# A reordered front end for a fused routed-attention and SwiGLU kernel: keys ahead of queries, odd-token one-hots put off, weights in column quarters, dummy products between the first exponentials

## The chip, the cores and the metric

The kernel runs on one core of one Trainium2 chip. The metric is the device time of one execution in microseconds (us). Every kernel was run several times. The profiles are single executions, and their spans are about 1.8 us shorter than the time of the same run, because the time includes a little before and after the span.

The engines in the profile are PE (TensorE's products), PEld (its weight loads), DVE (the vector engine), ACT (the scalar engine), POOL (GpSimd) and SP (the engine that here only issues transfers). "PEclk" is the clock granted to TensorE, 1.00 being full speed and 0.50 half speed.

## The reference

There are 4 batches, 8 heads, 768 tokens and a head width of 64. Each query and each key is assigned to one of 16 centroids of its head, by the largest cosine. A query attends only to keys with the same assignment. The result is normalised (RMS) and goes through a SwiGLU layer with 512 inputs and 1536 hidden columns.

```python
q_assign = argmax(einsum('bhsd,hcd->bhsc', q_n, c_n), axis=-1)   # k_assign likewise
mask = q_assign[:, :, :, None] == k_assign[:, :, None, :]
scores = where(mask, scale * q @ k.T, -1e9)
attn = softmax(scores) @ v
x = attn.transpose(0, 2, 1, 3).reshape(B * S, H * D)
xn = x / sqrt(mean(x * x) + 1e-6) * rms_g
out = (silu(xn @ w_gate) * (xn @ w_val)) @ w_out
```

## The kernel before

The mask costs no separate pass. To each query and key (64 rows after transposition) 16 more rows are added, a one-hot vector of the assignment, so that a product over 80 rows is large exactly where the assignments agree, and one exponential with a constant offset gives the masked weights. Producing these rows is the "preparation" of a head: load q and k, transpose them on TensorE (`trans`), copy to SBUF on ACT, multiply with the centroids (`scores_c`), find the maximum and compare on DVE, transpose back, and place the one-hots by a small DMA (`place`). `qcast` and `kcast` write the bf16 rows of query and key. Heads are prepared in groups of four.

The work is cut into 8 units, each half the tokens of one batch with all 8 heads. "Even" and "odd" tokens are the two halves; unit 0 uses only the even queries of batch 0, but all its keys. In unit u the attention of u runs (24 exponentials of 128x768), and beside it, as fill, the feed-forward work of earlier units and the preparation of later groups. The order of instructions on each engine is exactly the order of the program text.

```python
def load_gv(c):                       # gate and value weights, four row blocks
    nc.gpsimd.dma_start(out=wg[:, c], in_=moe_w_gate[c * P:(c + 1) * P])
    nc.gpsimd.dma_start(out=wv[:, c], in_=moe_w_val[c * P:(c + 1) * P])
...
def kcast(g, h, early=False):
    for e in range(2):
        to, of = kext[g % 4][:D, h, e * UQ:(e + 1) * UQ], qkT[g, h // 2][e * D:(e + 1) * D, h % 2, 1]
        if early:
            nc.scalar.activation(to, of, ACT.Copy, scale=1.0 / ZS)
        else:
            nc.vector.tensor_scalar_mul(to, of, 1.0 / ZS)
...
def group_work(g):                    # preparation of one group of four heads
    w = []
    for h in range(HG):
        ...
        def second(h=h, n=n):
            trans(g, h, 1)
            qcast(g, h)
            kcast(g, h)
            vcast(n)
            load_qk(n + NQ)
            load_v(n + NV)
        w.append((0.25, second))
...
def second_group():                   # runs between exponentials 2 and 3 of unit 0
    kcast(0, 2, True)
    kcast(0, 3, True)
    for m in range(2):
        scores_c(1, m)
    for c in range(CC):
        load_gv(c)
    ...
...
for u in range(NU):
    ...
    elif u == 1:
        prep = group_work(2) + group_work(3)
        fill += [(0.5, f) for _, f in prep[:8]] + ffn[:12] + [(0.0, output_weights)] + spread(ffn[12:], prep[8:])
    ...
            while n < len(fill) and (h, i) > (0, 0) and done <= total * (3 * h + i + 1) / gaps:
                done += fill[n][0]
                fill[n][1]()
                n += 1
```

The softmax here doesn't subtract the row's maximum and nothing guards it: scores larger than these inputs give would overflow.

## Time and profile before

| | before |
|---|---|
| time, median of 3 runs | 375.29 us (373.96 to 375.66) |
| profiled span | 371.76 us |
| first exponential | 18.82 us |
| last exponential of unit 0 ends | 44.81 us |
| normalised x of unit 0 complete | 53.55 us |
| first gate product | 58.40 us |
| key 11, the last load of group 2, lands | 51.41 us |
| starts of units 2 to 6 | 87.53, 129.85, 171.68, 213.51, 255.35 us |

These are lines of the page of the kernel before: the busy time of each engine with its instruction count; the busy share of TensorE and its clock in 40 slices of 9.3 us each (a digit 9 is 90% or more); the packets that the transfers were made of, by size; and two of the DMA issues, with the size of a transfer and the median time from issue to landing.

```profile
PE 351.1 (94%) x3026; PEld 210.5 (57%) x3026; DVE 241.7 (65%) x573; ACT 260.0 (70%) x461; POOL 107.6 (29%) x221
...
PE   7979867999999999999999999999999999999995
...
PEclk9976998999999999999999999999999999999999
...
DMA packets 24967, 32.03 MB, mean 86 GB/s; under 512 B 4960, under 2 KB 20832, under 8 KB 24928
...
wv<-in_moe_w_val_dram POOLq DMA_DIRECT2D x4, 384.0 KB, 10.3
wo<-in_moe_w_out_dram POOLq DMA_DIRECT2D x3, 512.0 KB, 13.5
```

Read the PE row first. From the eighth slice on TensorE is never under 90% but in the last one, so only the first seven slices, some 65 us, hold slack. The clock row has its own dip, in slices three and four (19 to 37 us), where the PE row shows 7 and 9: busy there means slow as well. The weight transfers are not urgent in this kernel: all gate and value weights are in by 44.54 us, and the output weights, issued at 55 us, are needed only in unit 2.

### The profile page before, as it was taken

What the parts mean: (1) busy time and instruction counts of PE and PEld (TensorE: products, weight loads), DVE (VectorE), ACT (ScalarE), POOL (GpSimd) and SP (SyncE); (2) the same over time, 40 slices, a digit from 0 to 9 for tenths busy, and PEclk for the clock granted to TensorE, in tenths of its full rate; (3) what the DMA queues carried; (4) which work ended last, traced back from release to release, by engine and by line L of the source; (5) the groups of instructions that cost most, each with busy time, mean ns of one, the idle gap of its engine ahead of it and who ended that gap; (6) DMA issues with size and microseconds to landing.
All of it is one profiled execution on the core that took longest, in us unless ns stands there. A gap on an engine that the chain in (4) does not pass through costs nothing.

```text
span 371.8 us, 8016 instructions
## 1 busy us (share of the span) xinstructions
PE 351.1 (94%) x3026; PEld 210.5 (57%) x3026; DVE 241.7 (65%) x573; ACT 260.0 (70%) x461; POOL 107.6 (29%) x221
## 2 busy tenths in 40 slices
PE   7979867999999999999999999999999999999995
PEld 3535544565566555655566555655566656664552
DVE  4981186678756966777756966777656565667432
ACT  4797983798669775888668775888767876762320
POOL 3694071089615170325315170325300000000000
PEclk9976998999999999999999999999999999999999
DMA  8649999726126101450022001000020002001002
GB/s 273 188 95 210 249 329 248 159 63 180 58 85 198 63 20 56 129 155 14 13 85 86 4 20 57 30 0 13 12 86 2 3 0 86 2 1 58 28 3 85
DMA packets 24967, 32.03 MB, mean 86 GB/s; under 512 B 4960, under 2 KB 20832, under 8 KB 24928
## 3 DMA queue, kind: packets, MB, share of 16 engines
q1 hardware_dynamic: 18288, 24.72, 20.5%
q0 software_dynamic: 6064, 6.00, 8.6%
q10 hardware_dynamic: 576, 0.79, 0.6%
q8 instruction: 24, 0.39, 0.4%
q14 instruction: 15, 0.12, 0.1%
HBM read 28.35 MB, written 6.29 MB: 93 GB/s over the span
## 4 chain that ended last, share of the span: by engine, by line
PE 71%; ACT 12%; DVE 11%; issue 3%; DMA 1%; DVEq 0%; SPq 0%; ACTq 0%
PE o L370 17%; PE gate L347 13%; PE val L347 13%; PE s L280 13%; PE acc L296 7%; ACT pT L282 7%; PE tq L196 3%; PE sc L251 3%; DVE th L356 2%; ACT th L355 2%; DVE kext L210 2%; ACT qkT L198 1%; ACT xn L315 1%; DVE oh L242 1%; DVE o_sb L373 1%
## 5 line engine op out<-in xcount | busy, mean ns | idle before, releaser
L282 ACT ACTIVATE pT<-s,off 128x768 bf16<-128x768 f32 x192 | 170.9, 902 | 48.3 <-PE s L280 47.3
L280 PE MATMUL s<-qext,kext 80*128 80x384 bf16 x384 | 96.6, 335 | 5.6 <-ACT pT L282 5.2
L347 PE MATMUL val<-xnT,wv 128*128 128x384 bf16 x384 | 78.7, 327 | 0.9 <-DVE th L356 0.6
L347 PE MATMUL gate<-xnT,wg 128*128 128x384 bf16 x384 | 78.9, 327 | 0.1
L370 PE MATMUL o<-wo,gvT 128*128 128x512 bf16 x288 | 70.3, 379 | 0.5
L356 DVE SCALAR_TENSOR_TENSOR th<-th,gate 128x384 f32<-128x384 f32 x84 | 46.4, 553 | 30.3 <-ACT th L355 29.2
L280 PEld LDWEIGHTS <-kext 80*128 80x128 bf16 x384 | 37.2, 100 | 45.2 <-issue 18.5
L202 POOL CAST qext<-qkT 64x384 bf16<-64x384 f32 x64 | 33.7, 526 | 97.2 <-ACT qkT L198 95.3
L355 ACT ACTIVATE th<-gate 128x384 f32<-128x384 f32 x84 | 41.2, 490 | 25.9 <-PE gate L347 22.0
L361 DVE SCALAR_TENSOR_TENSOR gvT<-th,val 128x384 bf16<-128x384 f32 x84 | 46.3, 552 | 9.1 <-PE val L347 2.6
L296 PEld LDWEIGHTS <-pT 128*128 128x128 bf16 x1152 | 44.9, 99 | 9.7 <-issue 0.8
L347 PEld LDWEIGHTS <-wv 128*128 128x128 bf16 x384 | 36.5, 98 | 23.7 <-issue 3.2
L347 PEld LDWEIGHTS <-wg 128*128 128x128 bf16 x384 | 36.6, 98 | 22.7 <-issue 0.7
L296 PE MATMUL acc<-vbf,pT 128*128 128x65 bf16 x1152 | 47.0, 195 | 0.5 <-ACT pT L282 0.5
L370 PEld LDWEIGHTS <-gvT 128*128 128x128 bf16 x288 | 26.7, 97 | 26.2 <-issue 1.0
L265 POOL DMA_DIRECT2D qext<-oh x56 | 27.2, 491 | 39.5 <-DVE oh L242 38.5
L196 PE MATMUL tq<-ident_f,qk 128*128 128x128 f32 x192 | 32.6, 289 | 3.1 <-DMA qk<-in_q_dram 1.2
L198 ACT COPY qkT<-tq 128x384 f32<-128x384 f32 x64 | 29.1, 484 | 5.8 <-PE tq L196 5.6
L210 DVE TENSOR_SCALAR kext<-qkT 64x384 bf16<-64x384 f32 x56 | 24.6, 440 | 12.0 <-ACT qkT L198 11.2
L196 PEld LDWEIGHTS tq<-ident_f,qk 128*128 128x128 f32 x192 | 22.8, 145 | 12.8 <-ACT qkT L198 3.2
L265 POOL DMA_DIRECT2D kext<-oh x48 | 23.3, 489 | 16.6 <-DVE inv L301 15.0
L373 DVE COPY o_sb<-o 128x512 f32<-128x512 f32 x24 | 16.4, 689 | 12.9 <-PE o L370 12.7
(60 smaller groups left out, 232.0 us busy)
## 6 DMA issues: line engine op xcount, KB each, us to landing
qk<-in_q_dram SPq DMA_DIRECT2D x32, 192.0 KB, 3.9
vs<-in_v_dram SPq DMA_DIRECT2D x32, 192.0 KB, 3.8
out_dram<-o_sb SPq DMA_DIRECT2D x24, 256.0 KB, 2.0
qk<-in_k_dram SPq DMA_DIRECT2D x28, 192.0 KB, 3.8
wg<-in_moe_w_gate_dram POOLq DMA_DIRECT2D x4, 384.0 KB, 9.1
wv<-in_moe_w_val_dram POOLq DMA_DIRECT2D x4, 384.0 KB, 10.3
wo<-in_moe_w_out_dram POOLq DMA_DIRECT2D x3, 512.0 KB, 13.5
qext<-oh POOLq DMA_DIRECT2D x56, 12.0 KB, 1.6
```

Of the source, the lines that this page charges most:

```text
L196: nc.tensor.transpose(ps[:, i * P:(i + 1) * P], qk[:, part, 2 * i:2 * i + 2].rearrange("p t d -> p (t d)"), ident_f)
L198: nc.scalar.copy(qkT[g, h // 2][:, h % 2, part], ps)
L202: nc.gpsimd.tensor_copy(qext[g % 4][:D, h, e * UQ:(e + 1) * UQ], qkT[g, h // 2][e * D:(e + 1) * D, h % 2, 0])
L265: on.dma_start(out=ext[D:D + NC, h, e * UQ:(e + 1) * UQ], in_=oh[32 * h + e * NC:32 * h + (e + 1) * NC])
L280: nc.tensor.matmul(ps[:, j, :UQ], lhsT=kext[g % 4][:KR, hh, kc * P:(kc + 1) * P], rhs=qext[g % 4][:KR, hh, hf * UQ:(hf + 1) * UQ], start=T ...
L282: nc.scalar.activation(pT[u, h][:, 2 * i:2 * i + 2], ps[:, :, :UQ], ACT.Exp, bias=off, scale=scale * ZS)
L296: nc.tensor.matmul(acc[:, h % 2, t], lhsT=pT[u, h][:, kc, t * P:(t + 1) * P], rhs=vbf[g % 4][:, hh, kc % HT * 2 + kc // HT], start=kc == 0 ...
L347: nc.tensor.matmul(ps, lhsT=w[:, c, f * P:(f + 1) * P], rhs=xnT[u][:, c], start=c == 0, stop=c == CC - 1)
L355: nc.scalar.activation(th, ps, ACT.Tanh, scale=0.5)
L356: nc.vector.scalar_tensor_tensor(th, th, 1.0, ps, op0=ALU.add, op1=ALU.mult)
L361: nc.vector.scalar_tensor_tensor(gvT[u][:, f], gates[u], 0.5, ps, op0=ALU.mult, op1=ALU.mult)
L370: nc.tensor.matmul(outs[u], lhsT=gvT[u][:, f, t * P:(t + 1) * P], rhs=wo[:, f], start=f == 0, stop=f == FC - 1)
```

## The change

The change rebuilds everything up to the middle of unit 1. Its parts, in the order in which the argument meets them:

1. Keys go first in the front end, so that their longer chain (cast, one-hot of all 768 keys) starts on the first data. The opening dummy products rise from 5 to 8.
2. Unit 0 needs only even queries. The casts and one-hots of the odd ones are put off behind the weights.
3. The gate and value weights come as four column quarters instead of four row blocks, and the output weights follow right behind them instead of in unit 1.
4. Key casts 2 and 3 of group 0 move from ACT to DVE, and a dummy product stands in every gap of unit 0 after the first head.
5. In unit 1 only the transposes of group 2 stay ahead of the first gate product. Its key casts go behind it, one token half per item of work.
6. The rule that spreads fill over the gaps now leaves out the first gap (`skip` = 1), and `spread` deals casts out in halves.

```diff
-    WARM = 5
+    WARM = 8
...
-    def load_gv(c):
-        nc.gpsimd.dma_start(out=wg[:, c], in_=moe_w_gate[c * P:(c + 1) * P])
-        nc.gpsimd.dma_start(out=wv[:, c], in_=moe_w_val[c * P:(c + 1) * P])
+    def load_gv(i):
+        c = slice(i * DF // 4, (i + 1) * DF // 4)
+        for w, of in ((wg, moe_w_gate), (wv, moe_w_val)):
+            nc.gpsimd.dma_start(out=w[:, :, c], in_=of[:, c].rearrange("(c p) f -> p c f", p=P))
...
+            t += [(0.3, lambda h=h: trans(g, h, 0)), (0.3, lambda h=h: trans(g, h, 1))]
+            def casts(h=h, n=n):
                 qcast(g, h)
-                kcast(g, h)
                 vcast(n)
                 load_qk(n + NQ)
                 load_v(n + NV)
+                kcast(g, h, es=(0,))
+            c += [(0.0, casts), (0.0, lambda h=h: kcast(g, h, es=(1,)))]
...
+    def second_clusters():
+        scores_c(1, 0)
+        one_hots(nc.sync, 0, (0, 1), (0,))
+        one_hots(nc.gpsimd, 0, (2, 3), (0,))
+        load_gv(0)
+        load_gv(1)
+        for n in range(HG, H):
+            vcast(n)
+        for i in range(2, 4):
+            load_gv(i)
+        for n in range(2, H):
+            qcast(n // HG, n % HG, (1,))
+        for g, h0 in ((0, 0), (0, 2), (1, 0)):
+            place(nc.sync, g, 0, h0, (1,))
         for c in range(0, FC, 4):
             load_o(c)
+
+    def more(h=None):
+        busy(1, False)
+        if h is not None:
+            kcast(1, h)
...
+            while n < len(fill) and at >= skip and done <= total * (at + 1 - skip) / (len(gaps) - skip):
...
+        if u == 1:
+            t, c, a = group_work(2)
+            fill, head, prep = [], t, c + a + group(3)
```

The many edits with `nt` and `UNITS` in the full diff only generalise the unit's size; all units still have three tiles.

## The prediction

> **What bounds the kernel now.** I first read the page for the whole span, then the same sums by stage, then the chain of waits inside the stage that stood out. The page says TensorE is busy 94% of 371.8 us, so what a change can win is the time in which TensorE is not both busy and at full clock. The sums by stage (columns: stretch in us; busy us and instruction count of PE, weight load, DVE, ACT, POOL; granted clock; DMA share; GB/s) show where that is:
>
> ```profile
> 18.82:45.20 26.38, 21.60 (x203) 12.00 (x202) 10.05 (x22) 23.44 (x35) 12.72 (x25) 0.81 0.85 178
> 23.80:34.00 10.20, 9.50 (x75) 5.54 (x73) 4.90 (x12) 7.40 (x10) 7.92 (x15) 0.51 0.78 141
> ...
> 45.20:58.40 13.20, 7.23 (x81) 5.28 (x80) 10.78 (x29) 8.96 (x22) 8.73 (x15) 0.99 0.99 314
> 54.50:58.10 3.60, 0.02 (x2) 0.02 (x1) 3.49 (x9) 0.60 (x1) 2.87 (x4) 1.00 1.01 296
> 58.10:61.60 3.50, 3.50 (x14) 1.73 (x14) 1.45 (x4) 1.39 (x2) 0.00 (x0) 0.51 1.09 231
> 58.40:87.10 28.70, 28.43 (x268) 16.86 (x266) 20.39 (x44) 23.02 (x39) 11.05 (x22) 0.94 0.59 133
> 170.00:212.00 42.00, 41.63 (x379) 25.65 (x378) 29.97 (x72) 31.79 (x57) 13.70 (x28) 1.00 0.14 44
> ```
>
> From 58.4 us on TensorE is 99% busy; only the first 58 us are loose. Unit 0 (the first half batch, its exponentials run from 18.82 to 44.81) is ACT's, except that the clock is halved from 23.8 to 34: there a pair of score products takes 0.64 us instead of 0.33. Unit 1 begins at 45.20 and reaches its first gate product at 58.40; 3.6 us of that TensorE stands still, and then runs cold for 3.5 us. The timeline shows what made it cold: ACT makes four key casts between the second and the third exponential, TensorE waits 2.2 us, and the next products are slow.
>
> ```profile
> 20.41 2.11 ACT L208 ACTIVATE kext<-qkT 64x384 bf16<-64x384 f32 x4
> 22.54 2.48 ACT L282 ACTIVATE pT<-s,off 128x768 bf16<-128x768 f32 x3
> ...
> 23.50 0.48 PE L280 MATMUL s<-qext,kext 80*128 80x384 bf16 x2 [2.20 <-ACT pT L282]
> 24.65 1.47 PE L280 MATMUL s<-qext,kext 80*128 80x384 bf16 x4
> ```
>
> And the chain of waits (start, us, what) explains the stop before 58.4: the normalised x is ready at 53.55, but eight key casts of the next batch stand ahead of its transposed copies on DVE.
>
> ```profile
> 51.58 1.97 DVE xn L327 x3
> 53.55 0.57 DVE kext L210
> ...
> 57.13 0.45 DVE kext L210
> 57.58 0.03 issue
> 57.61 0.43 DVE xnT L337
> 58.04 0.04 issue
> 58.08 0.44 PE tx L336 x3
> 58.52 1.32 PE gate L347 x4
> ```
>
> **What the Trainium skill says.** "TensorE: Matmul & The Clock Gate", Part 1, says that TensorE runs at half clock until it was active for a window of about 3.4 us and falls back after an idle one, with spacings N/1.2 GHz cold and N/2.4 GHz + 2.5 ns warm: for 384 columns 320 and 162 ns. The trace agrees (0.64 and 0.33 us a pair), and so do the two falls, after 2.2 us and 3.6 us of stillness. Part 4 of that page says transposes do not count as activity in the same way; the trace does not settle it: between 46.0 and 54.5 us transposes are about half the products and the clock stayed 1.00. "DMA: Bandwidth & Descriptors", section "Issuing engines are not separate DMA queues", says that all issuers share 16 engines. The trace agrees: with the output weights in flight the qk loads land 1.2 us apart (65.5 to 72.7 us), alone 0.52 us apart.
>
> **The change, part by part.** All durations are from the trace of before.
>
> *Before the first exponential.* Keys come first, so the first cluster chain on DVE (four steps of 0.58 us, 2.4 us) starts on key data. Eight opening dummies (0.43 us each, cold) end at 1.46 + 3.4 = 4.9 us; key 0 landed at 3.33, so the first transposes begin 0.6 us later than the 4.30 of now. TensorE's order up to the first score product is then: 36 transposes (0.42 us per three warm, 0.67 cold), cluster products 3 x 2 heads (0.8 us warm, 1.5 cold) and one of 4 heads (0.75), and 9 dummies (0.21). The first cluster product ends at about 8.4, its one-hots are ready at 11. From there, with the clock warm near 9 us: transposes of q0, q1, k2, k3 1.7, cluster 0.8, two dummies and q2, q3 with two more 1.7, two clusters 1.6 and about 0.8 waiting for ACT's casts (4 x 0.53) and copies, four key transposes with dummies 2.5, the cluster of group 1 0.8 and its wait for the last copy 0.3. The sum is 10.2, so 18.6 for the score product and 19.0 for the first exponential. Today it is 18.82: sixteen transposed copies became twelve, but the dummies (eight after the opening, 1.7 us) and a 4-head cluster were put in their place. So nothing is gained here.
>
> *Unit 0.* The four ACT casts (2.11 us) go to DVE, four copies (1.6 us, as eight take 3.18) stand there instead, and TensorE keeps 12 transposes and a cluster meanwhile. One dummy per gap costs 0.21 us; per head warm that is 6 x 0.163 + 0.54 + 0.64 = 2.2 us against ACT's 2.49, so it is hidden. If the clock holds, ACT sets the pace: 24 x 0.83 = 19.9, copies 1.6, two of the three squares 1.5, total 23.0, plus 0.5 for hitches. The last exponential ends at 19.0 + 23.5 = 42.5 instead of 44.81: 2.3 us won.
>
> *Unit 1 up to the first gate.* From the last exponential to the normalised x takes 53.55 - 44.81 = 8.7 us, a chain of squares and small DVE steps that is not touched: 51.2. The key casts now come after the first gate product, so 58.40 - 57.61 = 0.8 us later, at 52.0, the gate could start. I add 0.5 us because the transposes of group 2 wait for loads (see rivals): 52.5, or 5.9 us won.
>
> *Rest of unit 1.* It takes 87.15 - 58.40 = 28.75 today. No cold stretch: -1.7 (half of 3.5). One pair of score products fewer was done before the gate: +0.3. The eight casts (0.36 to 0.57 us) now lie in a stretch in which DVE has 20.4 + 3.3 + 1.4 (copies of the transposed x) busy of some 28: TensorE will wait for gate buffers a little, +1.0. So 28.4, ending at 80.9 instead of 87.15.
>
> *Everything after.* Units 2 to 7 and the end keep their operations; the casts are only split in two. 99% busy leaves nothing to win; I take 0. Weights in column quarters move the same bytes, and the first quarter suffices for three gate blocks, but before had all of them by 44.54, ahead of the need.
>
> The sum: 375.3 - 6.25 = 369.0 us.
>
> **The rivals.** *Loads become the bound.* Eight gate and value weight transfers take 2.05 us each now (30.07 to 44.54 us), and the output weights, 8 us of transfer, move from 55 us to right behind them, ahead of the second batch's loads, which start near 38. Shared evenly, key 11 lands at about 50 to 51 (51.41 now), just in time; shared as from 59 to 66 us today, where a load waited 5 us, it lands at 55 and the gate starts at 56.5: 372 to 373. *The clock falls anyway* near 24 us. For it: transposes and ACT-bound gaps are thin work. Against it: the wait of 2.2 us is broken up and the dummies begin with head 1, not head 4. It would cost about 3 us: 372. *DVE becomes unit 1's bound*, as it carries 25 us in order: 1 to 2 us more. *The front is quicker than I think*, because an earlier warm clock and fewer waits bring the first exponential to 17.5: 367.
>
> **Range and chances.** The first exponential is uncertain by 0.8 us either way, loads and clock together by +3, the DVE term by -1 to +1.5, the later units by 0.5 each way. That gives 365.5 to 372.5. The 2% line is 367.8, 1.2 us under my number, so faster 0.36; slower needs 8 us more than anything I found, 0.02.
>
> **What would show it.** First exponential between 18 and 20; no clock near 0.5 between 20 and 45; eight heads of unit 0 about 2.5 us apart after the first; the first gate product at 51 to 54 with the eight key casts behind it; TensorE busy 97% or more from there; units 2 to 5 still 41.8 to 42.3 us apart. A gate later than 55 behind a load, or a clock of 0.5 in unit 0, would prove me wrong towards 372; a first exponential before 18, towards 367.

## The result, and the profile after

The changed kernel takes 370.43 us (370.29 to 370.58, 4 runs), against 375.48 us (373.96 to 375.80, 4 runs) of the kernel before in the same rounds. The ratio is 0.9873 [0.9846, 0.9901], which counts as the same within 2%. Ratios here are the mean time of one kernel's runs over that of the other's of the same rounds, so not quite the ratio of the medians quoted. Executions over 1.5% slower than the fastest of the same kernel are left out of the means.

The page of the changed kernel, the same lines as before:

```profile
PE 351.6 (95%) x3047; PEld 213.0 (58%) x3047; DVE 237.0 (64%) x577; ACT 257.6 (70%) x457; POOL 108.4 (29%) x221
...
PE   8999669999999999999999999999999999999995
...
PEclk9999858999999999999999999999999999999999
...
DMA packets 28039, 32.03 MB, mean 87 GB/s; under 512 B 4960, under 2 KB 24928, under 8 KB 28000
...
wv<-in_moe_w_val_dram POOLq DMA_DIRECT2D x4, 384.0 KB, 11.0
wo<-in_moe_w_out_dram POOLq DMA_DIRECT2D x3, 512.0 KB, 23.8
```

The dip in the first four slices is gone from both rows, and a new one stands in slices five and six, from 37 to 55 us: TensorE has 6 and 6 where it had 8 and 6, and in the sixth the clock falls to 5 where it was 9. The hole was moved rather than closed. The row of packets shows what the column quarters did: the same 32.03 MB in 3072 more packets, 4096 more of them under 2 KB and 1024 fewer above it. The value weights still land after 11 us in the median, which hides what happened to them; the output weights take 23.8 us instead of 13.5.

The sums by stage of the changed kernel, to be held against those in the prediction (stretch; its length; busy us and count of PE, weight load, DVE, ACT, POOL; clock; DMA share; GB/s):

```profile
17.68:41.71 24.03, 21.05 (x218) 11.78 (x217) 12.85 (x26) 22.99 (x34) 19.54 (x34) 1.00 0.97 183
41.71:58.27 16.56, 11.07 (x80) 7.64 (x79) 5.86 (x21) 8.87 (x21) 6.52 (x12) 0.59 1.18 271
46.40:58.20 11.80, 9.00 (x54) 6.34 (x55) 3.19 (x12) 5.46 (x9) 4.95 (x10) 0.51 1.18 269
58.27:86.30 28.03, 27.32 (x270) 16.81 (x270) 23.17 (x54) 23.87 (x41) 14.98 (x30) 1.00 0.80 234
169.20:210.70 41.50, 41.24 (x380) 25.78 (x378) 28.74 (x72) 31.41 (x59) 13.74 (x29) 1.00 0.14 44
```

Unit 0 keeps its clock (1.00 for 0.81) and takes 24.03 us from its first exponential to the start of unit 1, for 26.38. The stretch up to the first gate product has grown from 13.20 to 16.56 us, at a clock of 0.59. The DMA share of 1.18 says that the engines are full there. The 271 GB/s, fewer than the 314 of before, do not show slower engines: they count bytes as they land, and the weights are read as float32 and land as bf16. The trace has 1113 weight packets of 768 bytes and 840 of 1024 in this stretch, beside 2.76 MB of loads; counted as read, with the weights doubled, that is some 374 GB/s (an estimate). The last row is a steady unit: it is 41.24 of 41.50 us busy and begins every 41.44 us, where it took 41.83.

The timeline of the same kernel names the waits (start in us, duration of the group, engine, line, operation, output and inputs, count, and in brackets the idle time before it and what ended it):

```profile
22.58 7.67 ACT L288 ACTIVATE pT<-s,off 128x768 bf16<-128x768 f32 x9 [0.55 <-PE s L284]
...
46.43 0.87 PE L200 MATMUL tq<-ident_f,qk 128*128 128x128 f32 x3 [1.53 <-DMA qk<-in_q_dram]
...
47.45 1.53 DVE L334 TENSOR_SCALAR xn<-x,ny 128x512 bf16<-128x512 f32 x3
...
49.72 0.87 PE L200 MATMUL tq<-ident_f,qk 128*128 128x128 f32 x3 [1.13 <-DMA qk<-in_q_dram]
...
55.85 0.42 DVE L345 TENSOR_SCALAR xnT<-tx,gcol 128x384 bf16<-128x384 bf16 x1 [6.88 <-PE tx L344]
...
58.27 0.97 PE L357 MATMUL gate<-xnT,wg 128*128 128x384 bf16 x4
```

The first row is the repaired part: nine exponentials one after another, with half a microsecond lost before the first of them. Then the new trouble. The normalised x is complete at 48.97 us, 4.6 us earlier than before, but its transposes stand behind the group-2 transposes (`tq`) on TensorE, and these wait for q and k. DVE sits idle for 6.88 us with x ready, and the gate starts at 58.27, almost exactly where it was (58.40). What the key casts had held is now held by loads. The durations show the fallen clock as well: three transposes take 0.87 us here and 0.52 in the kernel before.

| | before | after | gain |
|---|---|---|---|
| first exponential | 18.82 | 17.68 | 1.14 |
| first to last exponential of unit 0 | 25.99 | 23.65 | 2.34 |
| last exponential to normalised x | 8.74 | 7.64 | 1.10 |
| normalised x to first gate | 4.85 | 9.30 | -4.45 |
| first gate to the end of unit 1 | 28.75 | 27.69 | 1.06 |
| end of unit 1 to the end of the span | 284.61 | 282.65 | 1.96 |
| span | 371.76 | 368.61 | 3.15 |

The spans differ by 3.2 us and the medians by 5.05. The profiled run of the kernel before (373.53 us) is a little faster than all four of its timed runs, and over all the rounds that kernel ran anywhere from 370.96 to 375.80 us, while the four runs of the changed one lie within 0.3 us. So the stage table explains some 3 us, and about 2 us belong to this spread. A possible source of it was seen by chance: in experiment x4, whose front end is untouched, query 1 landed at 7.47 us instead of 5.64, the trace records the full clock from 12.57 us instead of 10.36, and the first exponential came at 20.53 instead of 18.82.

### The profile page after: what moved, and what is told of

The parts are those of the page before. It is cut to its first block, busy times and chain, and to the rows that moved or that the text cites. A ratio compares the mean times of both kernels' runs of the same rounds, so it can differ in the third digit from the quotient of the medians.

```text
span 368.6 us, 8061 instructions
## 1 busy us (share of the span) xinstructions
PE 351.6 (95%) x3047; PEld 213.0 (58%) x3047; DVE 237.0 (64%) x577; ACT 257.6 (70%) x457; POOL 108.4 (29%) x221
## 2 busy tenths in 40 slices
DMA packets 28039, 32.03 MB, mean 87 GB/s; under 512 B 4960, under 2 KB 24928, under 8 KB 28000
## 4 chain that ended last, share of the span: by engine, by line
PE 68%; DMA 9%; DVE 8%; ACT 5%; POOL 5%; issue 2%; SPq 1%; DVEq 0%; ACTq 0%
PE val L357 16%; PE gate L357 15%; PE o L379 12%; PE s L284 11%; DMA wo<-in_moe_w_out_dram 8%; PE acc L302 7%; PE tq L200 4%; ACT pT L288 3%; PE sc L255 2%; DVE o_sb L382 2%; ACT xn L322 2%; POOL qext L206 1%; DMA vs<-in_v_dram 1%; DVE xn L334 1%; PE warm L112 1%
## 5 line engine op out<-in xcount | busy, mean ns | idle before, releaser
L284 PE MATMUL s<-qext,kext 80*128 80x384 bf16 x384 | 94.6, 328 | 2.9 <-ACT pT L288 2.8
L366 DVE SCALAR_TENSOR_TENSOR th<-th,gate 128x384 f32<-128x384 f32 x84 | 46.3, 552 | 44.3 <-ACT th L365 43.9
L357 PEld LDWEIGHTS <-wg 128*128 128x128 bf16 x384 | 35.8, 97 | 24.4 <-issue 3.5
L302 PEld LDWEIGHTS <-pT 128*128 128x128 bf16 x1152 | 44.1, 98 | 9.3 <-ACT pT L288 0.6
L302 PE MATMUL acc<-vbf,pT 128*128 128x65 bf16 x1152 | 46.1, 194 | 0.5 <-ACT pT L288 0.5
L200 PE MATMUL tq<-ident_f,qk 128*128 128x128 f32 x192 | 33.9, 297 | 6.1 <-DMA qk<-in_q_dram 4.1
L268 POOL DMA_DIRECT2D qext<-oh x50 | 24.0, 488 | 39.5 <-DVE oh L246 39.5
L200 PEld LDWEIGHTS tq<-ident_f,qk 128*128 128x128 f32 x192 | 24.8, 151 | 14.8 <-issue 4.4
L214 DVE TENSOR_SCALAR kext<-qkT 64x384 bf16<-64x384 f32 x60 | 23.8, 397 | 2.3 <-ACT qkT L202 1.6
L345 DVE TENSOR_SCALAR xnT<-tx,gcol 128x384 bf16<-128x384 bf16 x32 | 12.3, 411 | 20.1 <-PE tx L344 20.1
## 6 DMA issues: line engine op xcount, KB each, us to landing
wo<-in_moe_w_out_dram POOLq DMA_DIRECT2D x3, 512.0 KB, 23.8
```

The costliest lines, as they stand in the source:

```text
L200: nc.tensor.transpose(ps[:, i * P:(i + 1) * P], qk[:, part, 2 * i:2 * i + 2].rearrange("p t d -> p (t d)"), ident_f)
L268: on.dma_start(out=ext[D:D + NC, h, e * UQ:(e + 1) * UQ], in_=oh[32 * h + e * NC:32 * h + (e + 1) * NC])
L284: nc.tensor.matmul(ps[:, j, :w] if nt == HT else flat[:, j * w:(j + 1) * w], lhsT=kext[g % 4][:KR, hh, kc * P:(kc + 1) * P], rhs=qext[g % ...
L302: nc.tensor.matmul(acc[:, h % 2, t], lhsT=pT[u, h][:, kc, t * P:(t + 1) * P], rhs=vbf[g % 4][:, hh, kc % HT * 2 + kc // HT], start=kc == 0 ...
L357: nc.tensor.matmul(ps, lhsT=w[:, c, f * P:(f + 1) * P], rhs=xnT[u][:, c, :n], start=c == 0, stop=c == CC - 1)
L366: nc.vector.scalar_tensor_tensor(th, th, 1.0, ps, op0=ALU.add, op1=ALU.mult)
```

## The experiments

Twelve kernels ran, four to a call, each with 3 timed rounds (4 runs each); all gave correct results. Every call has its own 7 runs of the kernel before (medians 373.74, 374.62 and 373.78 us), so kernels of different calls are compared by their ratios to it. On this scale the changed kernel is 0.9873.

**Theory A** was that the quarters hold the loads. A quarter is read in rows of 1536 bytes, as the q, k and v loads are, while the row blocks of before have rows of 6144 bytes (in float32, 384 and 1536 columns). The Trainium skill says in "DMA: Bandwidth & Descriptors", section "Queues, rings and completion order", that each transfer engine takes turns between its queues packet by packet. The trace of the changed kernel agrees: from 42 to 50 us, with both queues at work, 1008 weight packets and 920 load packets started, and each packet was one row. If so, the queue with long rows should get more of the engine, and with rows of one length both should get alike. **Theory B** was the rival: the output weights, moved ahead, hold the loads. The DMA issues in the traces gave the first hint. The eight quarter transfers (four of each matrix) land 1.4 to 4.1 us apart, the last at 52.83 us, where the row blocks landed 2.07 us apart on average, the last at 44.54.

**x1, output weights later.**

```diff
-        for c in range(0, FC, 4):      # end of second_clusters
-            load_o(c)
...
                 vcast(n)
+                if n == 3 * HG - 1:    # after the last v cast of group 2, in unit 1
+                    late_weights()     # the three load_o
```

> The changed kernel with only the three output-weight transfers issued later, behind the last v cast of group 2 in unit 1. Theory A (the gate and value quarters themselves, sharing the DMA engines evenly with the second batch's loads, delay key 11; the output weights wait behind them in the same software queue and only start at 52.8): key 11 still lands at 53.5 to 54.5, first gate at 57.5 to 58.5, 370.4 us +-0.6. Theory B (my recorded rival: the output weights moved ahead of the loads are the cause): key 11 lands by 51, first gate by 54, 366 to 367 us.

It took 368.98 us (368.43 to 369.60), ratio 0.9876 [0.984, 0.9912]. A new stop in unit 0 spoiled it, as its timeline shows:

```profile
32.25 0.48 PE L284 MATMUL s<-qext,kext 80*128 80x384 bf16 x2 [3.05 <-DMA qext<-oh]
```

A 12 KB one-hot transfer was issued by SP at 27.39 us, this time just after the first weight transfer (26.72 us), and landed 4.7 us later; in the changed kernel it went out at 26.58, just before the first weight transfer, and landed after 1.8 us. So unit 1 began 3.8 us late (45.47) and the loads had that much more time. Key 11 landed at 53.11 and the gate came at 56.2. The run separates nothing, and x12 below repeats it without the stop.

**x2, weights by rows.**

```diff
-        c = slice(i * DF // 4, (i + 1) * DF // 4)
         for w, of in ((wg, moe_w_gate), (wv, moe_w_val)):
-            nc.gpsimd.dma_start(out=w[:, :, c], in_=of[:, c].rearrange("(c p) f -> p c f", p=P))
+            nc.gpsimd.dma_start(out=w[:, i], in_=of[i * P:(i + 1) * P])
```

> The changed kernel with the gate and value weights again in four row blocks (128 rows of 6144 bytes) instead of column quarters (512 rows of 1536 bytes), issued at the same places. Theory A1 (the engines take turns row by row, so short rows halve the weights' share): the eight transfers land 2.1 us apart and are done at 44 to 46 as in the kernel before, the loads then come 0.55 us apart, key 11 at 50 to 51.5, first gate at 53.5 to 55, 366 to 367.5 us. Rival A2 (only the order and time of issue matter, not the row length): weights done at 52 to 53, key 11 at 54, gate at 58, 370.4 us.

It took 375.54 us (374.83 to 377.32), ratio 1.0067 [1.002, 1.0114], the slowest of all. Half of the expectation held: with rows of 6144 bytes the weights were in at 44.89. But they hardly met the loads. The one-hot stop struck here too (2.57 us) and made the loads late; their first packet started at 43.94 us, and only 35 load packets started before the last of those long rows was through. I had forgotten what comes next in the weight queue. The output weights followed at once (49.35, 54.21, 58.73 us) and held the loads: from 45 to 56 us 1200 of their packets started and 1091 of the loads', key 11 landed at 58.91 and the gate came at 62.7. So the run shows that output weights hold the loads as well when they come beside them. Whether long rows make the loads give way more was not tested, and rival A2, that order and time of issue decide, is not refuted.

**x3, half the weights later.**

```diff
-        for i in range(2, 4):          # in second_clusters
-            load_gv(i)
-        for c in range(0, FC, 4):
-            load_o(c)
...
+                if n == 3 * HG - 1:
+                    late_weights()     # quarters 3 and 4, then the three load_o
```

> The changed kernel with the third and fourth column quarters and the output weights issued behind the last v cast of group 2. Theory A (weights in flight beside the loads are the cause): the first two quarters are in by 39 to 40, the loads come about 0.55 us apart, key 11 lands at 45.5 to 47.5, first gate at 50 to 51.5, no cold clock between 46 and 58, 362.5 to 364.5 us. Rival C (the loads are late because of the ring or their own issue, or another wait such as the casts or the small DVE steps takes their place): first gate not before 55, 368 us or more. Rival D: the late quarters miss gate 6 near 72 us and TensorE waits there: gate early, time still above 367.

It took 365.06 us (364.51 to 365.22), ratio 0.9768 [0.9735, 0.9801]: about 4 us better than the changed kernel and 8.7 better than the one before. Its sums by stage, cut at the same events as above:

```profile
17.69:41.38 23.69, 21.10 (x218) 11.78 (x217) 12.86 (x26) 22.78 (x35) 14.11 (x27) 1.00 0.88 181
41.38:51.57 10.19, 6.85 (x79) 4.88 (x78) 6.95 (x21) 8.08 (x21) 6.70 (x13) 1.00 1.03 357
51.57:80.36 28.79, 27.42 (x271) 16.89 (x271) 23.69 (x54) 23.89 (x41) 11.97 (x22) 1.00 0.98 196
```

Only the second row differs much from the changed kernel: 10.19 us for 16.56, at a clock of 1.00 for 0.59, with 357 GB/s for 271. Key 11 landed at 46.43 and the gate started at 51.57, close to the 52.5 of my sum. The third row is 28.79 for 28.03 us, so a little of the gain went back. No one-hot stop struck here: between the first and the last, the heads of unit 0 are 2.5 to 2.6 us apart.

**x4, the kernel before with its casts behind the gate.**

```diff
                 qcast(g, h)
-                kcast(g, h)
+                if g != 2:
+                    kcast(g, h)
...
-            fill += [(0.5, f) for _, f in prep[:8]] + ffn[:12] + [(0.0, output_weights)] + ...
+            # the eight key casts of group 2, two each after the first four gate and value blocks
```

> The kernel before with one thing of the change: the eight key casts of group 2 are put behind the first gate products in DVE's order. If they held the first gate back as my prediction said: first gate at 54 to 55 instead of 58.4, no stop of 3.6 us, clock not at half from 58 to 61.6, time 4 to 5 us less than before (370.5 to 371.5). Rival: something else, a load or the transposes, holds the gate at 57 or later and the time falls less than 1.5 us.

It took 369.98 us (369.17 to 370.65), ratio 0.9901 [0.9865, 0.9938]. Two lines of its timeline:

```profile
7.60 0.87 PE L196 MATMUL tq<-ident_f,qk 128*128 128x128 f32 x3 [1.40 <-DMA qk<-in_q_dram]
...
56.71 1.00 PE L347 MATMUL gate<-xnT,wg 128*128 128x384 bf16 x4
```

The second line is 1.45 us behind the normalised x (55.26), where the kernel before needed 4.85, and there is no stop of TensorE. So the casts did hold the gate, as the prediction read from the chain. The first line is the late query 1 mentioned above, and it started everything 1.7 us late in this profile.

**x9, all one-hots ahead of the weights.** This is x3 with all group-1 query one-hots issued by POOL, so that their place in front of the weights no longer hangs on which of two issuers comes first. It is the base of the runs that follow.

```diff
-        one_hots(nc.sync, 0, (0, 1), (0,))
-        one_hots(nc.gpsimd, 0, (2, 3), (0,))
+        one_hots(nc.gpsimd, 0, (0, 1, 2, 3), (0,))
```

> The run with half the weights later (x3), and in addition the four query one-hots of group 1 (even tokens) all issued by POOL ahead of its first weight transfer, instead of two of them by SP at about the same time. In x1 and x2 the head-4 one-hots left SP after the first weight transfer, landed at 31 to 32 and stopped TensorE for 2.6 to 3.0 us; in the changed kernel they left just ahead of it. Expected: all four land by 29, heads of unit 0 never more than 2.7 us apart after the first, weights start 1 us later, first gate at 51 to 52.5, time 364.9 +-0.8 (as x3), so no harm and less risk. Rival: the weights' later start moves the loads and the gate beyond 53: 366 or more.

It took 365.16 us (364.87 to 365.63), ratio 0.9761 [0.9719, 0.9804], the same as x3 within the noise. The heads of unit 0 between the first and the last are 2.5 to 2.6 us apart, as in x3.

**x5, no dummy products in unit 0** (x9 without them):

```diff
     def more(h=None):
-        busy(1, False)
```

> x9 without the one dummy product in each gap of unit 0 (the opening eight and those ahead of the first exponential stay). Theory (ACT sets the pace and gaps between products are under 1 us): the clock stays at 1.00 through unit 0 and the time moves by less than 0.5 us. Rival (the dummies hold the clock): the clock falls to half somewhere between 22 and 38, a head then takes 3 us or more, unit 0 is 3 to 5 us longer and so is the time (368 to 370).

Its four runs took 364.19, 366.30, 364.77 and 370.73 us. The last counts as slow (1.8% above the fastest, at a mean granted clock of 0.967) and is left out; the ratio of the other three is 0.977 [0.9702, 0.9839]. In its profile the clock is 1.00 through unit 0, for example here:

```profile
23.00:30.00 7.00, 5.16 (x66) 2.97 (x65) 5.12 (x12) 6.96 (x10) 7.00 (x12) 1.00 0.53 87
```

TensorE is busy for 5.16 of 7.00 us and stays warm. The profiled run was the fastest of the four. So the dummies are not what made unit 0 faster in the fast runs. They are not hidden either: without them most heads are 2.4 us apart instead of 2.6, and the exponentials of unit 0 take 22.78 us instead of 23.47. Whether the slow one has to do with their absence is open: no profile of it was taken, and one run proves nothing.

**x6, five opening dummies** (x9 with `WARM = 5`).

> x9 with five opening dummies instead of eight. Theory (the eight, unbroken to the first transposes, bring the full clock by 7 us instead of 10 to 11): with five, the first cluster product of two heads takes 1.5 us or more instead of 1.1, the next transposes are cold too, and the first exponential comes at 18.5 to 19.5 instead of 17.6; time +0.8 to +1.8. Rival (the opening dummies only delay the first transposes): first exponential at 17.0 to 17.6, time the same or less.

It took 365.38 us (364.41 to 365.55), ratio 0.9761 [0.9717, 0.9804].

```profile
6.10 1.17 PE L255 MATMUL sc<-qkT,cblk 128*32 128x384 f32 x4 [0.40 <-ACT qkT L202]
```

The first cluster product starts at 6.10 us, and 1.17 us for four products is far from the cold duration (in the kernel before the first such group takes 2.12 us and the second, at 9.88 us, 1.47; warm ones take 0.88, 1.76 us for eight at 12.88). My theory that three more dummies buy the early clock is not borne out: the time did not change, and the gate came at 52.39. The first exponential even came 0.7 us earlier, at 17.0, but the five dummies need not be the reason: in x2, x5, x7, x8 and x12, with eight, it came at 17.0 to 17.1 as well. It goes with the moment from which the trace records the full clock: 4.2 to 5.3 us in these six profiles and in x11 (17.4), 6.1 to 6.9 in the changed kernel, x1, x3, x9 and x10 (17.6 to 17.7).

**x10, odd tokens early** (x9 with the odd casts and one-hots of groups 0 and 1 beside the even ones, as in the kernel before).

```diff
-        qcast(0, h, (0,))              # likewise for group 1, and in three place calls
+        qcast(0, h)
...
-        for n in range(2, H):
-            qcast(n // HG, n % HG, (1,))
-        for g, h0 in ((0, 0), (0, 2), (1, 0)):
-            place(nc.sync, g, 0, h0, (1,))
```

> x9 with the query casts and one-hots of the odd tokens made where those of the even tokens are, not put off behind the weights. Theory (what is put off frees POOL and SP for what unit 0 needs): POOL's two more placements and four more casts come ahead of the v casts, and the one-hots of groups 0 and 1 leave later; first exponential 0 to 0.6 us later, a head among 2 to 5 of unit 0 waits 1 to 3 us on one-hots or v casts, weights start 3 us later, time +2 to +4. Rival (POOL and SP had room): time within 0.7 us of x9.

It took 369.09 us (368.44 to 369.40), ratio 0.9863 [0.9819, 0.9906], so 3.9 us more than x9.

```profile
35.80 0.71 PE L302 MATMUL acc<-vbf,pT 128*128 128x65 bf16 x18 [2.29 <-POOL vbf L217]
```

The first exponential is unmoved (17.68), but POOL falls behind. Its v casts come late, TensorE waits 2.29 us for one, the weights go out 4.4 us later and unit 1 starts at 45.59 instead of 41.53. Unit 0 therefore needs the odd tokens put off, and the wait that shows it is for POOL.

**x7, the old fill rule** (x9 with the fill spread over all gaps).

```diff
-            while n < len(fill) and at >= skip and done <= total * (at + 1 - skip) / (len(gaps) - skip):
+            while n < len(fill) and at >= skip and done <= total * (at + 1) / len(gaps):
```

> x9 with the old rule of how much work goes into each gap between exponentials (before: share counted from gap 0 though gap 0 takes none, so the first gap that takes work takes a double share, four gate or value blocks in a row; after: counted from gap 1). Units 2 to 5 start 41.4 us apart in the changed kernel and 41.8 to 42.3 in the kernel before, which my prediction took as equal. Theory (the rule): units 2 to 5 are 41.7 to 42.3 us apart again, time +1.5 to +2.5 against x9. Rival (the divided casts or the order of the preparation): still 41.4, time as x9 within 0.6.

It took 368.60 us (368.18 to 368.76), ratio 0.9862 [0.9819, 0.9904], 3.4 to 3.8 us more than x9 (by the medians and by the ratios). The steady units are 42.22 us apart.

**x8, key casts undivided** (x9 with both halves of a key cast in one item).

```diff
-                kcast(g, h, es=(0,))
-            c += [(0.0, casts), (0.0, lambda h=h: kcast(g, h, es=(1,)))]
+                kcast(g, h)
+            c += [(0.0, casts)]
```

> x9 with the two key casts of a head again one item of work instead of two. Theory (the fill rule, not the casts, shortened the later units): units 2 to 5 stay 41.4 to 41.5 us apart, time as x9 within 0.6. Rival (undivided casts hold DVE 0.7 us and with it a gate buffer): 41.6 to 42 us apart, time +1 to +2.

It took 368.22 us (367.18 to 368.90), ratio 0.985 [0.9796, 0.9904]. The units are 42.12 to 42.16 us apart. Either part taken back alone gives units that are slower even than the 41.83 us of before; only with both do they take 41.44. Note what x8 does not separate: fewer items also change where `spread` puts the others, so it may be the shorter hold on DVE or the different places.

**x11, dummy products ahead of the gate** (x9 with four products between the last group-2 transpose and the transposes of x).

```diff
-            fill, head, prep = [], t, c + a + group(3)
+            fill, head, prep = [], t + [(0.0, lambda: busy(4, False))], c + a + group(3)
```

> x9 with four dummy products behind the last transposes of group 2, where TensorE waits 1.2 us for the first normalised rows and then runs its first gate and value products at half clock (52 to 54.6). Theory: the clock stays at 1.00 through 52 to 60, the rest of unit 1 is 0.6 to 1.2 us shorter, time 364.0 to 364.6. Rival (the waits between 49 and 51.8 are what drops it, or it is chance of the window): half clock all the same, time as x9.

It took 364.71 us (364.35 to 365.08), ratio 0.9759 [0.9717, 0.9801]. These are the sums by stage around the gate, first x9, then x11:

```profile
46.00:52.00 6.00, 3.79 (x41) 2.65 (x40) 4.73 (x12) 3.61 (x8) 5.63 (x11) 0.91 1.06 363
52.00:60.00 8.00, 8.00 (x64) 3.87 (x62) 6.44 (x17) 5.10 (x8) 4.51 (x7) 0.85 1.17 280
```

```profile
46.00:52.00 6.00, 4.57 (x46) 2.87 (x47) 4.76 (x12) 3.17 (x6) 5.63 (x11) 1.00 1.02 344
52.00:60.00 8.00, 7.23 (x67) 3.63 (x67) 6.98 (x16) 5.54 (x8) 4.18 (x6) 1.00 1.09 238
```

The clock dip of x9 (0.91 and 0.85, the first while its TensorE was only 63% busy) is gone in x11, and TensorE gets through the second stretch with 0.77 us to spare. The gate came at 51.29 us for 51.83. One profile does not prove that the dummies did it: x3, without them, kept 1.00 in its profile too. The mean clocks of the four runs (0.998 to 1.000, for 0.989 to 0.995 in x9 and 0.993 to 0.999 in x3) speak for them. The time is equal within the noise; it is the best median of all.

**x12, only the output weights later** (x1 with the one-hots of x9).

> x1 made clean: the changed kernel with the output weights later and the group-1 query one-hots all ahead of the weights, so that unit 0 does not stall; all four gate and value quarters stay early. It splits the load wait between the quarters and the output weights. If the quarters alone hold the loads (they are ahead in the same queue, and landed at 52.8 in the changed kernel while key 11 landed at 54.5): key 11 at 51.5 to 53.5, gate at 54.5 to 57, 367 to 369 us. If the output weights did: key 11 by 49, gate by 52.5, 365 us as x3 and x9.

It took 369.17 us (368.63 to 370.06), ratio 0.9881 [0.9837, 0.9925], the same as the changed kernel. Two rows of its sums by stage:

```profile
41.00:46.00 5.00, 2.08 (x27) 1.51 (x25) 2.94 (x12) 3.32 (x11) 1.59 (x3) 0.91 1.20 274
46.00:52.00 6.00, 4.17 (x16) 2.29 (x14) 2.36 (x7) 3.03 (x6) 3.06 (x6) 0.50 1.19 281
```

No stop spoils unit 0 this time (unit 1 starts at 40.91 us), and still the DMA engines are full at 270 to 280 GB/s and the clock falls to 0.50. The last four of the eight quarter transfers landed at 42.09, 46.18, 50.26 and 54.32 us, key 11 at 52.96, and the gate came at 56.42. With the output weights out of the way the quarters alone hold the loads: theory A holds and theory B falls as the main cause. From the start of unit 1 the gate took 15.5 us here, 16.6 in the changed kernel and 10.2 in x3, so the output weights added about 1 us. In the changed kernel they share the queue of the quarters, and their first packet started at 50.1 us, when the quarters were nearly through.

Five of the kernels (x3, x9 and, built on it, x5, x6 and x11; ratios 0.976 to 0.977) beat both. Their intervals reach across the 2% line, so whether they are faster than the kernel before by over 2% stays unclear, but they are 1% faster than the changed kernel (0.9873).

## Why the prediction was right or wrong

The predicted time was 369.0 us and the measured one 370.43, within the range; the most likely class, the same within 2%, came. But the number was reached by steps that erred in opposite directions.

**Before the first exponential: right in its size, too slow by 1.3 us.** I took the clock as warm near 9 us. The trace of the changed kernel records it as full from 6.67 us (before: 10.36), and the first cluster product, at 6.82, took 1.12 us for four products. The rival "the front is quicker than I think" named the cause and the size (17.5; measured 17.68). That eight dummies bring the early clock is not shown: x6 has it with five, at 4.38 us. How far the clock comes early is in part luck of the execution, as the profiles listed under x6 show. With keys first a late query 1 does less harm (x11: landed at 7.42 us, first exponential at 17.41).

**Unit 0: right.** 23.5 us predicted, 23.65 measured, heads 2.5 to 2.6 us apart, clock 1.00. The reason given was only half of it. x10 shows that the relief of POOL by the put-off odd tokens is needed, which the working did not count. x5 shows the clock holding without the dummies too, and its heads, 2.4 us apart, show that the dummies are not "hidden". What kept the clock was the removal of the 2.2 us wait. Three runs put such a wait back into unit 0 without meaning to, with all dummies in place (x1 3.05, x2 2.57, x10 2.29 us), and each time the clock fell to half within 1.6 us of its end (at 33.45, 31.75 and 37.32 us).

**Last exponential to normalised x: 8.7 us predicted, 7.64 measured.** I called the chain of small steps untouched, and it is: it takes 8.73 to 8.75 us in the nine experiments whose loads were not held up (x3 to x11). It is shorter only where they were: 7.64 in the changed kernel, 7.67 in x2, 7.98 in x12, 8.27 in x1. With late loads POOL has less to cast beside the chain (2.62 us of casts in its DVE part, for 4.99 before). Over all traces, scaling one 128x512 block of x on DVE takes 0.48 us with no POOL cast beside it (297 cases) and 0.71 with one all along (34 cases). So this gain is a by-product of the late loads.

**Up to the first gate: the step that failed.** It reads "I add 0.5 us because the transposes of group 2 wait for loads: 52.5", and the gate came at 58.27. The removal of the casts from the path was right, as x4 and x3 show (1.45 and 1.84 us from x to gate). The loads took their place. My rival "Loads become the bound" had nearly the size (key 11 at 55, gate at 56.5; measured 54.48 and 58.27) and the wrong carrier. It spoke of the output weights; x12 takes these off and the loads stay late; x3 puts off two of the quarters as well, and the gate comes at 51.57. I wrote that quarters "move the same bytes", with the last in by 44.54 before, and did not ask when. They were issued 1.5 us later and in two batches (26.96 to 29.21 and 31.83 to 34.03 us, for 25.44 to 29.38 before), and the loads, which wait for unit 0, 3.5 us earlier (37.35 for 40.83). So in the changed kernel the two met from 41.2 us on, and before for only 1.6 us (42.7 to 44.3). While both queues were busy a quarter transfer took 4.1 us, where row blocks alone took 2.07, and a q, k or v load landed every 1.15 us on average where it takes 0.52 alone. Whether the shorter rows add to this is not shown (see x2).

**Rest of unit 1: right in direction.** 28.4 predicted, 27.69 measured, clock 1.00. Part of this is owed to the late gate. Counted up to the start of unit 2 it takes 28.07 us here, while x3 and x9, with their early gates, take 28.79 and 28.95, near the 29.13 of before. So some of what an early gate wins is given back.

**The clock: one reading of the page was too quick.** I wrote that both falls of the kernel before agree with an idle window of 3.4 us. The second does (TensorE busy 0.06 of the 3.41 us before the fall at 58.15), the first does not: in the 3.41 us before the fall at 24.01, TensorE was busy for 1.21. The last section has what all traces show.

**Everything after: I took 0, it was 1.96.** Units 3 to 5 went from 41.83 to 41.44 us. "99% busy leaves nothing to win" overlooked that 1% of 280 us is 3. x7 and x8 show that the fill rule and the divided casts (or the places that `spread` then gives the rest) are both needed.

Added up from the table: the step to the gate should have won 3.55 us (4.85 to 1.3) and lost 4.45, so 8.0 us are missing there. The other steps gave 4.9 more than I expected (one of them, the 1.1, only because the loads were late): 1.3 before the first exponential, 1.1 to the normalised x, 0.7 in the rest of unit 1 and 2.0 after it, less 0.15 in unit 0. The remaining 1.9 us are the difference between the gain in the profiles (3.15) and in the medians (5.05), the spread of the kernel before. That the total came out near is therefore partly luck.

## What to carry to other kernels

When a wait is taken off a path, look at what the freed engine waits for next, and above all at the transfers: check what is in flight in every queue at that moment, and in which order. A faster stage can bring its loads forward into transfers that they used to miss. Weights that are not needed yet should be issued behind the loads that are; half of them, and the output weights, issued behind those loads were worth 4 us here. A page's chain line needs a check before it is believed: the chain of the changed kernel gives 8% to the output weights, because their landing at 66.79 us coincides with a DVE instruction that had no idle time before it.

## What the Trainium skill lacked or had wrong

- "DMA: Bandwidth & Descriptors", sections "Issuing engines are not separate DMA queues" and "Queues, rings and completion order", say that all issuers share the same engines and that each engine takes turns between queues packet by packet. The runs agree (1008 and 920 packets from 42 to 50 us), but the page has no figure for what two full queues do to each other. Here a quarter transfer took 4.1 us beside the loads and the loads came 1.15 us apart, against some 2.07 us for a row block alone and 0.52 for a load alone.
- The same page has nothing on small transfers behind large ones. A 12 KB one-hot transfer landed after 1.8 us when it was issued just ahead of the first weight transfer (26.58 against 26.96 us, changed kernel), and after 4.7 us when issued 0.67 us behind it on another queue (x1).
- "TensorE: Matmul & The Clock Gate", Part 1, puts the fall of the clock after an idle window of about 3.4 us, and speaks of frequent short idles without a measure. In the 14 traces here the changes of the clock lie whole multiples of 3.413 us apart, and cut into such windows they show that a window need not be idle. All 16 falls follow one in which TensorE was busy 56% or less (2% to 1.91 of 3.41 us); all 1394 windows at full clock that kept it were busy 57% or more (1.95 of 3.41 us and up). So the changed kernel fell at 44.22 us after a window that was half busy, x9 at 50.96 after 43%, and x3 kept 1.00 because its worst window had 57%. The busy times are those of the profile, whose product ends are modelled, so the border is only as exact as they are. For the rise no such border comes out.
- Part 4 of that page says that transposes do not count as activity in the same way. For keeping the clock they counted here: in x7 TensorE was busy 63% of the window from 42.23 to 45.65 us, but only 11% without the transposes, and the clock stayed at 1.00.
- Part 1 of that page warns that the clock events of a trace can be unreliable, but no page says that a trace can lack them at its start. The views give 1.00 for the first 10 us of the kernel before, but the packed trace has no record ahead of 10.36 us, and four cluster products took 2.12 us at 7.00 and 1.47 at 9.88 us, where eight took 1.76 at 12.88. A clock of 1.00 ahead of the first record means nothing.
